# The later chunks' scores head by head, with the three products of the split parts stacked in one contraction of 120 rows

## The chip, the cores and the metric

The kernel runs on one core of a Trainium2 chip. The metric is the device time of one execution in microseconds (us). Before the change three timed executions gave 582.05 us as the median, from 581.89 to 585.11. A change of 1% (5.8 us) or more is called faster or slower here.

The engines are named as in the profile: PE is TensorE (PEld its weight loads), DVE is VectorE, ACT is ScalarE, POOL is GpSimd, and SP is SyncE, which here issues nearly all DMA transfers.

## The reference

The program is an mLSTM layer followed by a gated feed-forward layer (FFN). Batch is 4, heads 8, sequence 768, head width 40; the FFN goes from 320 to 1536 and back.

```python
for t in range(S):                        # per batch and head
    m_new  = maximum(f_gate[t] + m, i_gate[t])
    f_stab = exp(f_gate[t] + m - m_new);  i_stab = exp(i_gate[t] - m_new);  m = m_new
    C = f_stab * C + i_stab * outer(v[t], k[t])
    n = f_stab * n + i_stab * k[t]
    y[t] = sigmoid(o_gate[t]) * (C @ q[t]) / maximum(abs(n . q[t]), 1.0)
x   = y.transpose(0, 2, 1, 3).reshape(B * S, H * D)      # 3072 x 320
out = (sigmoid(x @ w_gate) * (x @ w_val)) @ w_out
```

The weights arrive as 64-bit floats, and the kernel decodes them on the chip.

## The kernel before, in words

The sequence is cut into 6 chunks of 128 steps. A chunk of one batch row is a unit, so there are 24 units, written (chunk, row). Within a unit the recurrence is a masked attention: the scores are k against q over the 40 columns of a head, multiplied by a matrix of decays `d` (128 x 8 heads x 128), and `av` is their product with v. Between chunks the state C goes on in `cst`; its share of a unit's output is `in`, its update `cs`. When the four units of a chunk are done, their rows `xh`/`xl` go through the FFN: `pg` (two products, up) and `po` (down), in 12 slices of 128 of the 1536. The FFN of a chunk runs while the units of the next chunk are worked on, so PE's queue is a mixture of both.

A unit has five stages. `st_a` transposes q and k on PE into PSUM (`pt`, three groups of 3, 3 and 2 heads, so 120, 120 and 80 partitions) and prepares the operands of the scores. `st_b` makes the scores `s` and multiplies them into `d`. `st_c` makes `in`, `av` and the normalisation, `st_d` transposes the result for the FFN (`xt`), and `st_e` updates the state. The next loads of q, k, v, o and d are issued in `prefetch`, after `st_c` and `st_e` of a unit.

Accuracy is got by splitting numbers: a float32 value is a high part in the format fp32r, which PE multiplies in one pass, and a low part, the rest. A product of two split numbers is high by high, low by high and high by low. Chunks 0 and 1 make their scores in plain float32 (line 405 of the profile). Chunks 2 to 5, 16 units, use the split: `kh` (ACT, L374) and `kl` (DVE, L375) hold both transposed operands. Since a group holds three heads on 120 partitions, the q side is spread into a block matrix with zeros by a mask, `bh` on DVE and `bl` on POOL (L382), 384 or 256 columns wide; three products per group, nine per unit, add up in PSUM (L413).

The order of the work is written out in numbers: `PARAM['pos']` gives each stage and each weight step a position in units of FFN slices, `PARAM['open']` does so for the opening (chunk 0, rows 0 and 1). Events are issued in the order of these positions, and stages a to d with a small priority over the FFN work around them. Each engine's queue is executed in its order; a wait at its head holds what stands behind.

Buffers that matter: `kh`, `kl`, `bh` and `bl` exist once each, q, k, v, o and `d` three times, the two PSUM banks `pa` serve all of a unit's products.

Of the kernel before, what the change touches and what calls it, by code (L numbers as in the profile page):

```python
# [9 lines left out]
F32 = mybir.dt.float32  # L10
F32R = mybir.dt.float32r
# [42 lines left out]
    'ce': -6.41,  # L54
    'open': {
# [9 lines left out]
        'xt0': 66.039, 'wve': 68.058, 'wrb': 58.626, 'nb1': 61.591, 'wrc': 61.877, 'xt1': 48.778, 'wrd': 70.574,  # L65
        'wre': 69.0, 'kw1': 69.362, 'e2': 87.005,
# [7 lines left out]
def mlstm_then_gated_ffn_kernel(  # L74
# [15 lines left out]
    P = 128  # L90
# [251 lines left out]
    def st_a(c, b):  # L342
# [21 lines left out]
        kh = two.tile([P, 3, 2, L], F32R, tag="kh", name=f"kh_{c}_{b}", bufs=1)  # L364
        kl = two.tile([P, 3, 2, L], F32R, tag="kl", name=f"kl_{c}_{b}", bufs=1)
        bh = two.tile([P, 3, 3, L], F32R, tag="bh", name=f"bh_{c}_{b}", bufs=1)
        bl = two.tile([P, 3, 3, L], F32R, tag="bl", name=f"bl_{c}_{b}", bufs=1)
        sop[u] = kh, kl, bh, bl
        for g, (h0, nh) in enumerate(GROUPS):
# [4 lines left out]
            nc.scalar.activation(kh[:r, g], pt[:r], AF.Copy)  # L374
            nc.vector.tensor_tensor(kl[:r, g], pt[:r], kh[:r, g].bitcast(F32), ALU.subtract)  # L375
            if c > 0:
                if PARAM["eng"].get(f"qk{g}") == "a":
                    nc.scalar.activation(qk[u][:r, g], pt[:r, 0], AF.Copy)
                else:
                    nc.vector.tensor_copy(qk[u][:r, g], pt[:r, 0])  # L380
            for eng, src, dst in ((E(f'bh{g}'), kh, bh), (E(f'bl{g}'), kl, bl)):
                eng.tensor_tensor(dst[:r, g, :nh, :],  # L382
                                        src[:r, g, 0, :].bitcast(F32).unsqueeze(1).broadcast_to([r, nh, L]),
                                        bmask[:r, :nh, :], ALU.mult)
# [514 lines left out]
```

## Time and profile before

| | value |
|---|---|
| timed executions, median (range) | 582.05 us (581.89 to 585.11) |
| the profiled execution's own time | 587.93 us |
| its span, first to last instruction | 586.2 us |
| granted PE clock, mean | 0.98 |
| instructions | 9768 |
| PE, PEld busy | 555.0 us, 506.0 us |
| DVE, ACT, POOL busy | 370.9, 234.3, 213.3 us |
| DMA moved | 43.91 MB, mean 75 GB/s |

The profile is one execution. A matmul's end is modelled, and matmuls are pipelined: one that lasts 0.34 us in a row may be followed 0.18 us later by the next. What one costs PE is therefore read from the start of one row to the start of the next. A row of the timeline gives start, duration, engine, line, operation, what it writes and reads, shapes, and a count where equal rows were merged. In rows of groups the two numbers after the bar are the busy time of the group in us and the mean of one in ns; then come idle time before them and what ended it. A float32 product shows as two instructions, an fp32r product as one.

### The profile page before, as it was taken

Reading aid. Unit: us, or ns where it says so; the run is one execution under the profiler, and the core shown is the slowest. Engines: PE = TensorE matmul, PEld = TensorE weight load, DVE = VectorE, ACT = ScalarE, POOL = GpSimd, SP = SyncE. Lnnn points to the kernel's source line nnn. Section 1 sums busy time; section 2 is a strip of 40 time slices with the busy share of each in tenths; the row PEclk is TensorE's granted clock in tenths of the full one; section 3 lists DMA queues with packets and bytes.
Section 4 is the critical chain, followed back from the end, with each engine's and each line's share of the span. In section 5 each row is a group of like instructions: output and inputs, shape, how many; then the busy total and the mean of one; then the engine's idle time right before and its main releaser. Section 6 shows DMA issues by size and latency. Waiting matters only on the chain.

```text
span 586.2 us, 9768 instructions
## 1 busy us (share of the span) xinstructions
PE 555.0 (95%) x3601; PEld 506.0 (86%) x3601; DVE 370.9 (63%) x780; ACT 234.3 (40%) x580; POOL 213.3 (36%) x279
## 2 busy tenths in 40 slices
PE   8639989899999999999999999999999999999997
PEld 7528878688999998999888988898888889999996
DVE  4697877966446786665767656676656767533322
ACT  5375757445335334343332342333342322223222
POOL 5566644654234543533445323445312321000000
PEclk9777999999999999999999999999999999999999
DMA  9875765322403405312030523030423000010000
GB/s 200 238 180 154 172 206 129 93 82 46 112 15 77 109 13 130 81 45 70 13 82 11 128 64 74 13 82 13 119 66 81 1 1 1 0 46 1 25 1 22
DMA packets 112847, 43.91 MB, mean 75 GB/s; under 512 B 101280, under 2 KB 104544, under 8 KB 112800
## 3 DMA queue, kind: packets, MB, share of 16 engines
q1 hardware_dynamic: 111712, 43.04, 30.0%
q8 instruction: 28, 0.46, 0.3%
q10 hardware_dynamic: 1088, 0.26, 0.2%
q14 instruction: 19, 0.16, 0.1%
HBM read 39.26 MB, written 4.03 MB: 74 GB/s over the span
## 4 chain that ended last, share of the span: by engine, by line
PE 80%; DVE 9%; DMA 3%; ACT 3%; POOL 2%; issue 2%; POOLq 0%; ACTq 0%; DVEq 0%
PE pg L509 31%; PE po L533 7%; PE po L532 7%; PE po L531 6%; PE av L429 5%; PE pg L511 5%; PE pg L514 5%; PE s L413 4%; DMA st_o<-in_moe_w_out_dram 2%; PE in L424 2%; PE pt L373 2%; PE cs L477 2%; DVE dc L266 2%; DVE dc L261 1%; PE xt L465 1%
## 5 line engine op out<-in xcount | busy, mean ns | idle before, releaser
L509 PE MATMUL pg<-xh,wh 128*128 128x256 f32 (+1 forms) x412 | 116.8, 350 | 3.8 <-ACT sg L516 2.2
L516 ACT ACTIVATE sg<-pg 128x256 f32<-128x256 f32 (+1 forms) x103 | 48.2, 468 | 169.9 <-PE pg L514 169.2
L517 DVE SCALAR_TENSOR_TENSOR sg<-sg,pg 128x256 f32<-128x256 f32 (+1 forms) x103 | 53.9, 523 | 97.6 <-ACT sg L516 93.1
L509 PE MATMUL pg<-xh,wl 128*128 128x256 f32 (+1 forms) x412 | 112.1, 342 | 0.0
L509 PE MATMUL pg<-xl,wh 128*128 128x256 f32 (+1 forms) x412 | 107.6, 334 | 0.0
L532 PE MATMUL po<-ol,gh 128*128 128x320 f32 x288 | 96.7, 336 | 0.0
L533 PE MATMUL po<-oh,gl 128*128 128x320 f32 x288 | 95.0, 330 | 0.0
L531 PE MATMUL po<-oh,gh 128*128 128x320 f32 x288 | 94.2, 327 | 0.4 <-ACT gh L520 0.4
L509 PEld LDWEIGHTS pg<-xh,wh 128*128 128x128 f32 x412 | 71.5, 192 | 11.0 <-ACT sg L516 3.8
L521 DVE TENSOR_TENSOR gl<-sg,gh 128x256 fp32r<-128x256 f32 (+1 forms) x103 | 62.5, 607 | 27.7 <-ACT gh L520 26.9
L509 PEld LDWEIGHTS pg<-xl,wh 128*128 128x128 f32 x412 | 70.9, 191 | 7.1
L509 PEld LDWEIGHTS pg<-xh,wl 128*128 128x128 f32 x412 | 70.8, 192 | 6.6
L520 ACT ACTIVATE gh<-sg 128x256 fp32r<-128x256 f32 (+1 forms) x103 | 51.7, 502 | 46.6 <-DVE sg L517 46.2
L382 POOL TENSOR_TENSOR bl<-kl,bmask 120x384 fp32r<-120x384 f32 (+1 forms) x48 | 50.3, 1056 | 54.7 <-DVE kl L375 54.7
L531 PEld LDWEIGHTS po<-oh,gh 128*128 128x128 f32 x288 | 54.7, 190 | 3.2 <-ACT gh L520 0.6
L532 PEld LDWEIGHTS po<-ol,gh 128*128 128x128 f32 x288 | 54.6, 190 | 0.9 <-issue 0.3
L533 PEld LDWEIGHTS po<-oh,gl 128*128 128x128 f32 x288 | 54.3, 189 | 0.5 <-DVE gl L521 0.2
L429 PEld LDWEIGHTS av<-v,d 128*128 128x128 f32 x352 | 52.7, 192 | 1.5 <-PE in L424 0.9
L511 PE MATMUL pg<-xh,w 128*128 128x256 f32 (+1 forms) x206 | 52.8, 332 | 0.0
L514 PE MATMUL pg<-xl,w 128*128 128x256 f32 (+1 forms) x206 | 52.3, 332 | 0.0
L429 PE MATMUL av<-v,d 128*128 128x41 f32 x352 | 50.7, 254 | 0.8 <-issue 0.8
L382 DVE TENSOR_TENSOR bh<-kh,bmask 120x384 fp32r<-120x384 f32 (+1 forms) x48 | 46.3, 965 | 0.0
(134 smaller groups left out, 914.2 us busy)
## 6 DMA issues: line engine op xcount, KB each, us to landing
d<-mscr SPq DMA_DIRECT2D x22, 512.0 KB, 3.8
k<-in_k_dram SPq DMA_DIRECT2D x24, 160.0 KB, 3.3
v<-in_v_dram SPq DMA_DIRECT2D x24, 160.0 KB, 3.6
o<-in_o_gate_dram SPq DMA_DIRECT2D x24, 160.0 KB, 3.7
st_o<-in_moe_w_out_dram SPq DMA_DIRECT2D x12, 320.0 KB, 3.2
out_dram<-ob SPq DMA_DIRECT2D x24, 160.0 KB, 1.8
q<-in_q_dram SPq DMA_DIRECT2D x23, 160.0 KB, 2.5
st<-in_moe_w_gate_dram SPq DMA_DIRECT2D x6, 512.0 KB, 4.5
```

The lines of the kernel that those rows point to most:

```text
L382: eng.tensor_tensor(dst[:r, g, :nh, :], src[:r, g, 0, :].bitcast(F32).unsqueeze(1).broadcast_to([r, nh, L]), bmask[:r, :nh, :], ALU.mult)
L429: nc.tensor.matmul(pv[:, h, :], dm[u][:, h, :], vt[u][:, h, :], start=True, stop=True)
L509: nc.tensor.matmul(pg[n], w[n][:, a, fs], x[c][:, a, n0:n1], start=(i + a == 0), stop=False)
L511: nc.tensor.matmul(pg[n], w2[n][:, fs], xh[c][:, 2, n0:n1], start=False, stop=False)
L514: nc.tensor.matmul(pg[n], w2[n][:, fs], xl[c][:, 2, n0:n1], start=False, stop=True)
L516: nc.scalar.activation(sg, pg[0], AF.Tanh, scale=0.5)
L517: nc.vector.scalar_tensor_tensor(sg, sg, 1.0, pg[1], ALU.add, ALU.mult)
L520: last = nc.scalar.activation(gh[u][:, :nt], sg, AF.Copy)
L521: E('gl0' if c == 0 else 'gl').tensor_tensor(gl[u][:, :nt], sg, gh[u][:, :nt].bitcast(F32), ALU.subtract)
L531: nc.tensor.matmul(po[t], g1[:, ts], oh[:, j, :], start=(j == 0), stop=False)
L532: nc.tensor.matmul(po[t], g1[:, ts], ol[:, j, :], start=False, stop=False)
L533: nc.tensor.matmul(po[t], g0[:, ts], oh[:, j, :], start=False, stop=(j == NF - 1))
```

## The change: what it does

For chunks 2 to 5 the block matrices are no longer made. `kh` and `kl` are laid out with the operand (q or k) ahead of the group. Two new tiles, `ks` and `qs`, are filled by DMA from SBUF to SBUF: for a head, 40 partitions of the high part of k, below them the same 40 again, below them 40 of the low part; for q the order is high, low, high. One product over 120 partitions then gives high by high plus high by low plus low by high. It is 128 columns wide, one per head, eight per unit. The transfers are 18 per unit (three parts, three places of a head in its group, two operands), 40 partitions by 1536 or 1024 bytes, all issued by SP.

```diff
 PARAM = {
     'pos': {
-        'e0': -11.132, 'a0': -4.375, 'b0': -13.304, 'a1': -17.116, 'e1': -7.942, 'c0': -10.313, 'd0': -8.526, 'b1':
+        'e0': -4.126, 'a0': -3.256, 'b0': -13.366, 'a1': -17.116, 'e1': -6.935, 'c0': -10.823, 'd0': -9.886, 'b1':
...
-    'ce': -6.41,
+    'ce': -3.09,
...
-        kh = two.tile([P, 3, 2, L], F32R, tag="kh", name=f"kh_{c}_{b}", bufs=1)
-        kl = two.tile([P, 3, 2, L], F32R, tag="kl", name=f"kl_{c}_{b}", bufs=1)
-        bh = two.tile([P, 3, 3, L], F32R, tag="bh", name=f"bh_{c}_{b}", bufs=1)
-        bl = two.tile([P, 3, 3, L], F32R, tag="bl", name=f"bl_{c}_{b}", bufs=1)
-        sop[u] = kh, kl, bh, bl
+        kh = two.tile([P, 2, 3, L], F32R, tag="kh", name=f"kh_{c}_{b}", bufs=1)
+        kl = two.tile([P, 2, 3, L], F32R, tag="kl", name=f"kl_{c}_{b}", bufs=1)
         for g, (h0, nh) in enumerate(GROUPS):
...
-            nc.scalar.activation(kh[:r, g], pt[:r], AF.Copy)
-            nc.vector.tensor_tensor(kl[:r, g], pt[:r], kh[:r, g].bitcast(F32), ALU.subtract)
...
-            for eng, src, dst in ((E(f'bh{g}'), kh, bh), (E(f'bl{g}'), kl, bl)):
-                eng.tensor_tensor(dst[:r, g, :nh, :],
-                                        src[:r, g, 0, :].bitcast(F32).unsqueeze(1).broadcast_to([r, nh, L]),
-                                        bmask[:r, :nh, :], ALU.mult)
+            nc.scalar.activation(kh[:r, :, g, :], pt[:r], AF.Copy)
+            nc.vector.tensor_tensor(kl[:r, :, g, :], pt[:r], kh[:r, :, g, :].bitcast(F32), ALU.subtract)
...
+        ks = two.tile([P, H, L], F32R, tag="bh", name=f"ks_{c}_{b}", bufs=1)
+        qs = two.tile([P, H, L], F32R, tag="bl", name=f"qs_{c}_{b}", bufs=1)
+        sop[u] = ks, qs
+        for x, dst, parts in ((1, ks, (kh, kh, kl)), (0, qs, (kh, kl, kh))):
+            for i, p in enumerate(parts):
+                for m in range(3):
+                    ng = len(range(m, H, 3))
+                    nc.sync.dma_start(dst[i * D : (i + 1) * D, 3 * m : 3 * m + ng, :].bitcast(F32),
+                                      p[m * D : (m + 1) * D, x, :ng, :].bitcast(F32))
...
-        kh, kl, bh, bl = sop.pop(u)
+        ks, qs = sop.pop(u)
         for g, (h0, nh) in enumerate(GROUPS):
-            r = nh * D
             ps = bank(c, b, [P, 3, L], f"s_{g}")
-            for i, (x, y) in enumerate(((kh, bh), (kl, bh), (kh, bl))):
-                nc.tensor.matmul(ps[:, :nh, :], x[:r, g, 1, :], y[:r, g, :nh, :], start=(i == 0), stop=(i == 2))
+            for m in range(nh):
+                nc.tensor.matmul(ps[:, m, :], ks[: 3 * D, 3 * m + g, :], qs[: 3 * D, 3 * m + g, :], start=True, stop=True)
```

Most numbers of `pos` and `open` are others too, so the order moves everywhere. In what follows a name's last number tells buffers apart, the numbers ahead of it are chunk and row (for `pg` chunk, slice and first row).

PE's queue before, at the scores of unit (4,3), amid the up products of slice 10:

```order
L509 MATMUL pg_3_10_0_4683<-xh_3361,wh_99 128x512
L477 MATMUL cs_2_4626<-v_2_3859,k_2_3858 120x123
L413 MATMUL s_4_3_4655<-bh_3_4535,kh_3_4533 128x384
L413 MATMUL s_4_3_4655<-bh_3_4535,kl_3_4534 128x384
L413 MATMUL s_4_3_4655<-bl_3_4536,kh_3_4533 128x384
L509 MATMUL pg_3_10_0_4683<-xh_3361,wh_99 128x512
```

The same place now:

```order
L510 MATMUL pg_3_10_0_4814<-xl_3652,wh_96 128x512
L414 MATMUL s_4_3_4788<-qs_3_4638,ks_3_4637 128x128
L414 MATMUL s_4_3_4793<-qs_3_4638,ks_3_4637 128x128
L414 MATMUL s_4_3_4788<-qs_3_4638,ks_3_4637 128x128
L414 MATMUL s_4_3_4793<-qs_3_4638,ks_3_4637 128x128
L510 MATMUL pg_3_10_0_4814<-xl_3652,wh_96 128x512
```

Three products of 384 columns made one group; now two groups are made in turn, head by head. Between the last `pt` of this unit and its first score stand 24 products `po`, 21 `pg` and the `in`, `av` and `cs` of unit (4,2).

DVE's queue before, in stage a of unit (4,0):

```order
L375 TENSOR_TENSOR kl_0_4008<-pt_4_0_4011,kh_0_4007 120x256
L380 COPY qk_0_4006<-pt_4_0_4011 120x128
L382 TENSOR_TENSOR bh_0_4009<-kh_0_4007,bmask 120x384
L521 TENSOR_TENSOR gl_1_0_4003<-sg_1_0_3999,gh_1_0_4002 128x512
L375 TENSOR_TENSOR kl_0_4008<-pt_4_0_4019,kh_0_4007 120x256
```

And now:

```order
L372 TENSOR_TENSOR kl_0_4047<-pt_4_0_4048,kh_0_4046 120x2x128
L538 TENSOR_SCALAR ob_0_4089<-po_2_3126 128x320
L376 COPY qk_0_4045<-pt_4_0_4048 120x128
L522 TENSOR_TENSOR gl_0_0_4039<-sg_0_0_4035,gh_0_0_4038 128x512
L372 TENSOR_TENSOR kl_0_4047<-pt_4_0_4054,kh_0_4046 120x2x128
```

The product with the mask is gone from the row of steps between one group and the next.

SP's queue before, where the output rows `ob` of chunk 2 leave:

```order
L133 DMA v_2_3859<-in_v_dram 128x8x40
L541 DMA out_dram<-ob_1_3966 128x320
L541 DMA out_dram<-ob_0_3960 128x320
L541 DMA out_dram<-ob_2_3972 128x320
L541 DMA out_dram<-ob_3_3978 128x320
L131 DMA q_3_4134<-in_q_dram 128x8x40
```

And now, with the transfers of unit (4,0):

```order
L133 DMA v_2_3947<-in_v_dram 128x8x40
L385 DMA ks_0_4066<-kh_0_4046 40x256 x2
L542 DMA out_dram<-ob_0_4089 128x320
L385 DMA qs_0_4067<-kh_0_4046 40x256
L542 DMA out_dram<-ob_1_4095 128x320
L385 DMA ks_0_4066<-kh_0_4046 40x384 x3
L542 DMA out_dram<-ob_2_4101 128x320
L385 DMA ks_0_4066<-kh_0_4046 40x384
L542 DMA out_dram<-ob_3_4107 128x320
L385 DMA ks_0_4066<-kl_0_4047 40x384 x2
L385 DMA ks_0_4066<-kl_0_4047 40x256
L385 DMA qs_0_4067<-kh_0_4046 40x384 x2
```

Six more transfers to `qs` follow behind the piece shown, and the load of q of unit (4,3) comes after them. In this unit the output's transfers stand among the new ones; in most others the 18 stand in a block.

More of the change, by code (lines that the diff above doesn't have):

```diff
@@ L53 @@
     'pin': 2.71,
-    'ce': -6.41,
+    'ce': -3.09,
     'open': {
[9 rows of a table removed]
-        'xt0': 66.039, 'wve': 68.058, 'wrb': 58.626, 'nb1': 61.591, 'wrc': 61.877, 'xt1': 48.778, 'wrd': 70.574,
-        'wre': 69.0, 'kw1': 69.362, 'e2': 87.005,
[9 rows of a table added]
+        72.38, 'xt0': 65.463, 'wve': 69.125, 'wrb': 54.301, 'nb1': 62.627, 'wrc': 63.052, 'xt1': 50.168, 'wrd':
+        71.641, 'wre': 79.377, 'kw1': 70.535, 'e2': 88.072,
     },
@@ L373, in st_a @@
                 nc.tensor.transpose(pt[:r, x, :], t[u][:, h0 : h0 + nh, :].rearrange("p h d -> p (h d)"), ident)
[L374 to L380, printed above, removed]
-            for eng, src, dst in ((E(f'bh{g}'), kh, bh), (E(f'bl{g}'), kl, bl)):
-                eng.tensor_tensor(dst[:r, g, :nh, :],
-                                        src[:r, g, 0, :].bitcast(F32).unsqueeze(1).broadcast_to([r, nh, L]),
-                                        bmask[:r, :nh, :], ALU.mult)
+            nc.scalar.activation(kh[:r, :, g, :], pt[:r], AF.Copy)
+            nc.vector.tensor_tensor(kl[:r, :, g, :], pt[:r], kh[:r, :, g, :].bitcast(F32), ALU.subtract)
+            if PARAM["eng"].get(f"qk{g}") == "a":
+                nc.scalar.activation(qk[u][:r, g], pt[:r, 0], AF.Copy)
+            else:
+                nc.vector.tensor_copy(qk[u][:r, g], pt[:r, 0])
+        ks = two.tile([P, H, L], F32R, tag="bh", name=f"ks_{c}_{b}", bufs=1)
[7 more added lines that the diff above has]
+                                      p[m * D : (m + 1) * D, x, :ng, :].bitcast(F32))
     dlast = {}
```

46 rows, old and new, of the table PARAM are left out of this document.

## The prediction

> **What bounds the kernel now.** I read the busy shares and the chain first. In the chain the columns are shares of the span.
>
> ```profile
> PE 555.0 (95%) x3601; PEld 506.0 (86%) x3601; DVE 370.9 (63%) x780; ACT 234.3 (40%) x580; POOL 213.3 (36%) x279
> PE 80%; DVE 9%; DMA 3%; ACT 3%; POOL 2%; issue 2%; POOLq 0%; ACTq 0%; DVEq 0%
> PE pg L509 31%; PE po L533 7%; PE po L532 7%; PE po L531 6%; PE av L429 5%; PE pg L511 5%; PE pg L514 5%; PE s L413 4%; DMA st_o<-in_moe_w_out_dram 2%; PE in L424 2%; PE pt L373 2%; PE cs L477 2%; DVE dc L266 2%; DVE dc L261 1%; PE xt L465 1%
> ```
>
> PE carries 80% of the path; the scores to be changed (L413) are 4% of it, 23.4 of 586.2 us, or 1.46 us for each of 16 units. DVE's 9% must lie somewhere, so the busy times by stretch come next; the columns are start and end, length, then busy time per engine, granted clock, DMA share and GB/s.
>
> ```profile
> 30.00:40.00 10.00, 2.92 (x20) 2.07 (x19) 9.62 (x22) 7.73 (x28) 4.36 (x8) 0.84 0.92 210
> 50.00:100.00 50.00, 47.00 (x304) 40.72 (x304) 40.12 (x93) 33.06 (x91) 24.86 (x32) 1.00 0.65 170
> 100.00:150.00 50.00, 47.38 (x275) 40.93 (x274) 33.90 (x65) 25.50 (x61) 27.15 (x29) 1.00 0.32 83
> 190.00:250.00 60.00, 56.34 (x426) 54.55 (x425) 44.35 (x106) 21.67 (x61) 29.59 (x39) 0.97 0.36 83
> 250.00:300.00 50.00, 50.00 (x334) 46.10 (x334) 32.07 (x72) 18.20 (x42) 19.29 (x24) 1.00 0.18 41
> 300.00:400.00 100.00, 99.85 (x585) 88.41 (x584) 64.79 (x127) 36.13 (x81) 39.11 (x49) 1.00 0.27 65
> 400.00:500.00 100.00, 100.00 (x589) 88.96 (x589) 69.19 (x132) 31.73 (x66) 28.90 (x34) 1.00 0.18 41
> ```
>
> From 250 to 500 us PE is busy 249.85 of 250 us: there only less work on PE shortens anything. From 190 to 250 it stands idle 3.66 us at a clock of 0.97. In the opening DVE is full (9.62 of 10) and PE mostly waits. The waits of PE in 200 to 250, and the opening's largest, are (us in total, times, longest):
>
> ```profile
> PE s L413 <- DVE xl L468: 1.3, 1, 1.3
> PE s L413 <- DVE qk L380: 0.9, 1, 0.9
> PE xt L465 <- DVE qk L380: 0.7, 1, 0.7
> PE pt L354 <- ACT cst L489: 4.8, 2, 3.7
> ```
>
> **The scores on PE.** What a product costs PE is the step from its start to the next start. This stretch at 442 us has no gaps (start, duration):
>
> ```profile
> 439.73 0.62 PE L509 MATMUL pg<-xh,wh 128*128 128x512 f32 x2
> 440.19 0.63 PE L509 MATMUL pg<-xh,wl 128*128 128x512 f32 x2
> ...
> 442.06 0.34 PE L413 MATMUL s<-bh,kh 120*128 120x384 f32 x1
> 442.24 0.31 PE L531 MATMUL po<-oh,gh 128*128 128x320 f32 x1
> 442.39 0.34 PE L413 MATMUL s<-bh,kl 120*128 120x384 f32 x1
> 442.57 0.31 PE L532 MATMUL po<-ol,gh 128*128 128x320 f32 x1
> ...
> 444.18 0.29 PE L413 MATMUL s<-bh,kh 80*128 80x256 f32 x1
> 444.31 0.31 PE L532 MATMUL po<-ol,gh 128*128 128x320 f32 x1
> ...
> 445.40 0.90 PE L424 MATMUL in<-cst,qk 120*128 120x123 f32 x6
> 446.14 1.92 PE L429 MATMUL av<-v,d 128*128 128x41 f32 x16
> 447.88 0.71 PE L509 MATMUL pg<-xh,wh 128*128 128x512 f32 x2
> ```
>
> A score product of 384 columns costs 0.18 us (442.06 to 442.24), one of 256 some 0.125, `po` 0.15, `pg` of 512 columns 0.23. A unit's nine are 6 x 0.18 + 3 x 0.125 = 1.455 us, which agrees with the chain's 1.46. The new product, 128 columns with a weight load of its own each time, does not occur in fp32r. Two bounds: by columns alone, the step from 384 to 256 saves 0.055, so 128 would cost 0.07; among small products, sixteen of 41 columns take 1.74 us, 0.109 each, and six of `in` (123 and 82 columns) 0.74 us, 0.123 each. Three times fewer columns cost the same there, so columns do not set it; each brings new weights. I take 0.11, from the nearest in kind: 8 x 0.11 = 0.88 us. Saved: 0.575 us per unit, times 16, **-9.2 us**, all on the path. At 0.07 it is -14.3. [...]
>
> **DVE and POOL.** Gone with the masks, per unit (mean ns before the last bar):
>
> ```profile
> L382 POOL TENSOR_TENSOR bl<-kl,bmask 120x384 fp32r<-120x384 f32 x32 | 37.8, 1184 | 49.8 <-DVE kl L375 49.8
> L382 DVE TENSOR_TENSOR bh<-kh,bmask 120x384 fp32r<-120x384 f32 x32 | 33.8, 1057 | 0.0
> L382 DVE TENSOR_TENSOR bh<-kh,bmask 80x256 fp32r<-80x256 f32 x16 | 12.5, 783 | 0.0
> ```
>
> DVE loses 2 x 1.06 + 0.78 = 2.9 us and POOL about 3.2 us per unit. After 250 us that buys nothing, since PE does not wait. Before it, the three waits above (2.9 us) end on DVE steps that stand behind `bh`, and the lower clock costs 0.03 x 60 = 1.8 us. At most 4.7 us come back; at least nothing, if the waits pass to ACT. I take **-2.5**. `kh`, `kl` and `qk` stay, at the same sizes.
>
> **The transfers.** A unit's path from `pt` to the scores now runs through 18 issues of SP. Nearest rows, for a transpose, `kh`, an ACT step that can stand ahead of it, SP's spacing and the landing (KB over all issues, then us):
>
> ```profile
> L373 PE MATMUL pt<-ident,k 128*80 128x128 f32 x16 | 4.3, 271 | 0.0
> L374 ACT ACTIVATE kh<-pt 80x256 fp32r<-80x256 f32 x16 | 6.0, 375 | 8.6 <-PE pt L373 8.6
> L227 ACT ACTIVATE d<-d 128x1024 f32<-128x1024 f32 x16 | 16.7, 1047 | 1.3 <-POOL d L226 1.3
> 302.13 0.37 SPq L132 DMA_DIRECT2D k<-in_k_dram  x1
> 302.55 0.69 SPq L133 DMA_DIRECT2D v<-in_v_dram  x1
> 38.38 2.24 SPq L169 DMA_DIRECT2D mscr<-mg  x4
> d<-mscr SPq DMA_DIRECT2D x22, 512.0 KB, 3.8
> out_dram<-ob SPq DMA_DIRECT2D x24, 160.0 KB, 1.8
> ```
>
> The first issue comes 0.65 us after the start of the last transpose (0.27 + 0.375), 1.7 us with the ACT step ahead. `kl` follows on DVE while the first six, from `kh`, are issued. Seventeen steps of 0.42 us (302.13 to 302.55) are 7.1. Landing is between 1.8 (160 KB) and 3.8 us (512 KB); these carry 61 KB or 41 KB. The whole is 9.6 to 12.6 us. Cover: for unit (4,3), 24 `po`, 21 `pg` of 512 columns and unit (4,2)'s `in`, `av` and `cs` (28 instructions at about 0.11) stand between, 24 x 0.15 + 21 x 0.23 + 28 x 0.115 = 11.6 us. Counted so, all 16 gaps are 11.3 to 15.5 us, ten of them at 12.2 or less. A chain of 9.6 is hidden; one of 12.6 leaves about 8 us of waits in all. I take **+2**, mostly for rows 0 of chunks 3 to 5, whose transfers share SP with the outputs. Queued behind SP's waits are loads for later units, which are not needed before the next units begin, and the outputs; an output that leaves late holds one of two buffers that `ob` shares with `t1`, and so DVE and ACT, which is why these rows 0 are where I put the waits.
>
> [...]
>
> **The order.** Stages a of chunk 2 start about three slices earlier within chunk 1, which is needed for the longer path. In the opening the transposes of unit (0,2), which wait 4.8 us above for a PSUM bank, now stand behind the gates' transposes; DVE stays full, so I take **-1**, between -4.8 and +4.
>
> **Sum.** -9.2 - 2.5 + 2 - 1 = -10.7 us. The profiled execution took 587.93 us (span 586.2) and would take 577.2. The median of the timed ones is 582.05, 5.9 us below it; the difference is carried over: **571.4 us**.
>
> **The rivals.**
>
> *Cheaper products.* At 0.07 the scores give -14.3: 566.3 us. For it: weight loads overlap with a long `pg` ahead. Against: the 0.109 of `av`. [...] Chance 0.15.
>
> *Late transfers (slower).* If SP spaces its issues as in the opening's row of four (2.24 us, 0.56 each, at a DMA share of 0.92), and ACT delays the first and landing takes 3.8, the path is 1.7 + 17 x 0.56 + 3.8 = 15.0 us, and the 16 gaps leave about 40 us of waits; with a landing of 1.8, a path of 13.0 us, about 13 us. It decides from 12.7 us of waits on (all gains but the transfers' own term), 0.8 per unit, a path of about 13 us. For it: nothing is spare in the ten short gaps. Against: a DMA share of 0.18 to 0.36 there. The time is 582.05 - 12.7 + 13 = 582 to 609; I take the middle of the lower half, 592. Chance 0.12.
>
> *Dear products.* If PE takes fp32r of 128 columns as it takes float32, two steps of 0.123 (`in`), a unit costs 8 x 0.246 = 1.97, +8.2 us instead of -9.2: 588.8. For it: nothing of this width in one pass is in the trace. Against: 384 to 256 columns scale as expected. Chance 0.10.
>
> *Gain given back early.* Chunk 2's units now fall into the stretch 50 to 150 us as well, where PE already idles 5.6 us; if that doubles, 577. Chance 0.15.
>
> That the change doesn't do what it says is excluded: the queue shows 128 products of 128 columns and no mask step.
>
> **How the numbers follow.** The forecast has 0.48 (566 to 577). Faster by over 1% means below 576.2: nearly all of the forecast, the cheap products, a quarter of the last rival, 0.64. Slower means above 587.9: most of the late transfers, half of the dear products, 0.13. Within 1%: 0.23. The range goes from 562 (cheap products, all 4.7 us of DVE's waits, no wait for transfers: 566.3 - 2.2 - 2) to 587, leaving out about 0.05 below and 0.14 above.
>
> **What would show it.** Right: `s` (L414) steps of 0.11 us, 14 us of the chain; no masks; PE busy in nearly all of 250 to 500 us; no wait of `s` on a DMA above 1 us; last `qs` landing within 11 us of the last `pt`. Wrong: `s` waiting on `qs` or `ks` in many units, SP spacing above 0.5 us, or steps of 0.07 or 0.2 us.

## The result, and the profile after

| | before | after |
|---|---|---|
| median of 4 runs, us | 582.99 (581.89 to 585.11) | 650.33 (644.31 to 653.5) |
| ratio, with 95% interval | | 1.114 (1.104 to 1.123) |
| profiled execution, us (span) | 587.93 (586.2) | 652.26 (650.5) |
| PE busy, us | 555.0 | 585.4 |
| PE idle in the span, us | 31.2 | 65.1 |
| mean granted clock | 0.980 | 0.924 |

The forecast was 571.4 us, and the kernel became 67 us slower. The profile splits the 64.3 us between the spans into two nearly equal halves: PE stands idle 33.9 us longer, and it is busy 30.4 us longer, although it has less to compute. Some executions of a kernel take over 1.5% more than its fastest; the ratios in this document leave these out, the medians do not.

The page of the changed kernel, busy time, clock by slice and the chain's shares by engine and by line:

```profile
PE 585.4 (90%) x3585; PEld 528.3 (81%) x3585; DVE 324.5 (50%) x732; ACT 232.6 (36%) x580; POOL 158.0 (24%) x231
PEclk9669999999979988778898996989898989899999
PE 50%; SPq 17%; DVE 11%; DMA 9%; ACT 5%; issue 4%; POOL 4%; ACTq 0%; POOLq 0%; DVEq 0%
PE pg L510 18%; SPq L385 17%; PE av L430 4%; DMA qs<-kh 4%; PE po L534 4%; PE po L532 3%; PE po L533 3%; PE pg L512 3%; PE s L414 3%; PE pg L515 3%; PE in L425 2%; PE pt L370 2%; DMA st_o<-in_moe_w_out_dram 2%; DVE dc L266 1%; DMA o<-in_o_gate_dram 1%
```

PE's share of the chain fell from 80% to 50%; SP's issuing of the new transfers (L385) took 17%, and their landing (`qs<-kh`) 4%. Relief came where it was forecast and buys nothing: DVE is busy 324.5 us instead of 370.9, POOL 158.0 instead of 213.3.

The stretches, with the columns as before (start and end, length, busy time of PE, PEld, DVE, ACT and POOL, granted clock, DMA share, GB/s):

```profile
190.00:250.00 60.00, 55.52 (x410) 53.06 (x410) 30.89 (x81) 20.93 (x58) 14.81 (x22) 0.94 0.42 106
250.00:300.00 50.00, 44.86 (x261) 43.93 (x260) 18.36 (x51) 12.97 (x36) 7.27 (x12) 0.73 0.30 81
300.00:400.00 100.00, 91.81 (x495) 79.18 (x493) 42.60 (x92) 29.02 (x63) 18.88 (x30) 0.94 0.31 84
400.00:500.00 100.00, 92.52 (x499) 79.86 (x498) 44.83 (x98) 31.19 (x70) 18.96 (x28) 0.92 0.34 92
```

From 250 to 500 us PE was busy 249.85 us at full clock before; now it is busy 229.19 us, at a clock between 0.73 and 0.94. The waits of PE from 165 us on (us in total, times, longest):

```profile
PE s L414 <- DMA qs<-kh: 24.1, 15, 3.7
PE s L414 <- issue: 7.0, 5, 2.4
```

Thirteen of the sixteen later units wait at their first score product, for 1.4 to 3.7 us. What they wait for is SP. Its issues of the end of unit (4,0) (start, duration):

```profile
385.36 2.25 SPq L385 DMA_DIRECT2D ks<-kl  x3
387.65 1.46 SPq L385 DMA_DIRECT2D qs<-kh  x2
389.15 2.21 SPq L385 DMA_DIRECT2D qs<-kl  x3
391.41 2.21 SPq L385 DMA_DIRECT2D qs<-kh  x3
393.72 0.42 SPq L131 DMA_DIRECT2D q<-in_q_dram  x1
```

Three new transfers take 2.25 us (389.15 to 391.41 for three), 0.75 us each, while the load of q behind them takes 0.42. The 18 of a unit take 13.5 us. In all sixteen units the first score product stands 13.0 to 16.3 us behind the last transpose.

And what the clock does after such a wait; the stretch around unit (3,0)'s scores, in windows of 3 us:

```profile
281.00:284.00 3.00, 2.52 (x20) 2.31 (x18) 0.85 (x2) 0.80 (x2) 0.00 (x0) 1.00 0.21 75
284.00:287.00 3.00, 0.46 (x3) 0.49 (x3) 0.00 (x0) 0.00 (x0) 0.00 (x0) 0.77 0.22 77
287.00:290.00 3.00, 3.00 (x15) 3.00 (x16) 1.07 (x3) 0.39 (x1) 0.00 (x0) 0.50 0.35 67
...
296.00:299.00 3.00, 3.00 (x12) 2.66 (x12) 2.12 (x8) 1.51 (x6) 0.51 (x3) 0.50 0.90 254
299.00:302.00 3.00, 3.00 (x16) 2.39 (x15) 1.24 (x4) 0.76 (x2) 1.74 (x1) 0.96 0.52 85
```

PE waits 3.0 us and then works at a clock of 0.50 until 299 us, which costs another 6.4 us (half of the 12.7 us from 286.5 on). From 150 us on there are 14 idle stretches of 1.4 to 3.7 us, and 12 of them are followed by such a stretch, from 3.4 to 14 us long; together these cost some 36 us. Before, there was one stretch at half clock after 150 us, of 3.4 us.

### The profile page after: what moved, and what is told of

Same layout as the page of the kernel before. It is cut to its first block, busy times and chain, and to the rows that moved or that the text cites. A ratio compares the mean times of both kernels' runs of the same rounds, so it can differ in the third digit from the quotient of the medians.

```text
span 650.5 us, 10100 instructions
## 1 busy us (share of the span) xinstructions
PE 585.4 (90%) x3585; PEld 528.3 (81%) x3585; DVE 324.5 (50%) x732; ACT 232.6 (36%) x580; POOL 158.0 (24%) x231
## 4 chain that ended last, share of the span: by engine, by line
PE 50%; SPq 17%; DVE 11%; DMA 9%; ACT 5%; issue 4%; POOL 4%; ACTq 0%; POOLq 0%; DVEq 0%
PE pg L510 18%; SPq L385 17%; PE av L430 4%; DMA qs<-kh 4%; PE po L534 4%; PE po L532 3%; PE po L533 3%; PE pg L512 3%; PE s L414 3%; PE pg L515 3%; PE in L425 2%; PE pt L370 2%; DMA st_o<-in_moe_w_out_dram 2%; DVE dc L266 1%; DMA o<-in_o_gate_dram 1%
## 5 line engine op out<-in xcount | busy, mean ns | idle before, releaser
L510 PE MATMUL pg<-xh,wl 128*128 128x256 f32 (+1 forms) x412 | 119.2, 358 | 0.0
L510 PE MATMUL pg<-xl,wh 128*128 128x256 f32 (+1 forms) x412 | 115.5, 350 | 0.0
L522 DVE TENSOR_TENSOR gl<-sg,gh 128x256 fp32r<-128x256 f32 (+1 forms) x103 | 65.8, 639 | 35.3 <-ACT gh L521 34.9
L510 PEld LDWEIGHTS pg<-xh,wl 128*128 128x128 f32 x412 | 73.7, 199 | 6.0
L510 PEld LDWEIGHTS pg<-xl,wh 128*128 128x128 f32 x412 | 73.0, 198 | 5.7
L430 PEld LDWEIGHTS av<-v,d 128*128 128x128 f32 x352 | 59.6, 211 | 4.5 <-DVE t L427 0.9
L414 PEld LDWEIGHTS s<-qs,ks 120*128 120x128 f32 x128 | 25.2, 235 | 41.3 <-issue 37.8
L414 PE MATMUL s<-qs,ks 120*128 120x128 f32 x128 | 29.5, 322 | 31.7 <-DMA qs<-kh 24.1
L534 PEld LDWEIGHTS po<-oh,gl 128*128 128x128 f32 x288 | 56.1, 195 | 0.6 <-DVE gl L522 0.3
L430 PE MATMUL av<-v,d 128*128 128x41 f32 x352 | 54.1, 272 | 0.7 <-DVE t L427 0.7
```

Source lines behind the costliest of these rows:

```text
L414: nc.tensor.matmul(ps[:, m, :], ks[: 3 * D, 3 * m + g, :], qs[: 3 * D, 3 * m + g, :], start=True, stop=True)
L430: nc.tensor.matmul(pv[:, h, :], dm[u][:, h, :], vt[u][:, h, :], start=True, stop=True)
L510: nc.tensor.matmul(pg[n], w[n][:, a, fs], x[c][:, a, n0:n1], start=(i + a == 0), stop=False)
L522: E('gl0' if c == 0 else 'gl').tensor_tensor(gl[u][:, :nt], sg, gh[u][:, :nt].bitcast(F32), ALU.subtract)
L534: nc.tensor.matmul(po[t], g0[:, ts], oh[:, j, :], start=False, stop=(j == NF - 1))
```

## The experiments

Theory 1, formed from these lines: SP needs 0.75 us for each transfer where I took 0.42, so that the path is longer than the gap that the order leaves, PE waits, and each wait brings half clock. The rivals: the products of 128 columns or the new order are dear in themselves; or the transfers cost by what they hold up, and not by PE's wait for the last one. Ratios below are against the kernel before, run beside each variant. The order that a table of positions gives also depends on the instructions in it: less PE's waits, the scores of the changed kernel stand 11.2 to 15.2 us behind the last transpose, those of the products alone, with the same table, 0.4 to 18.4 us.

### The products alone

```diff
-        ks = two.tile(...);  qs = two.tile(...);  18 x nc.sync.dma_start(...)
+        sop[u] = kh
...
-                nc.tensor.matmul(ps[:, m, :], ks[: 3 * D, 3 * m + g, :], qs[: 3 * D, 3 * m + g, :], start=True, stop=True)
+                nc.tensor.matmul(ps[:, m, :], kh[: nh * D, 1, g, :], kh[: nh * D, 0, g, :], start=True, stop=True)
```

> The changed kernel without the eighteen transfers: the eight products of 128 columns read the transposed high parts where they lie (contraction over the 120, 120 and 80 rows of a group), so the low parts and the separation by head are left out of the scores. Theory 1 (the transfers arrive too late, because SP needs 0.707 us to issue one where I took 0.42 for the spacing, and PE stands waiting): without them the rest of my sum holds, 582 less 9.2 (products), 2.5 (masks) and 1 (order), that is 569 us, 563 to 577, and PE's busy time from 250 to 500 us is back at 249 of 250 us. Rival, dear products or a dear new order: the time stays above 590 us, since neither is touched. By the step between products this run also settles their price: 0.11 us each by my sum, 0.07 or 0.246 at its ends.

Measured: ratio 1.002 (0.996 to 1.008); median 590.8 us against 586.1, with ten executions from 581 to 595 us. Without the transfers nearly the whole loss is gone, so they carry some 11%. But my sum without them, 569, is missed as well: theory 1 is right on the transfers, and something else takes back what the products save. The next two runs separate that.

### The order alone, and the products in the old order

The first is the kernel before with the changed kernel's table of positions, the second the products alone with the table of the kernel before. Neither changes any other line.

> The kernel before with the changed kernel's table of positions: nine products, masks, no transfers, only the new order. The products alone took some 590 us (most of its runs), not my 569, and what it lost it lost before 200 us: PE was busy 125.2 of the first 150 us against 127.4 before, at a clock of 0.80, 0.97 and 0.93 against 0.80, 1.00 and 1.00. Theory A (the new order costs some 10 us by itself, in the opening): 588 to 597 us, with the same rows up to 150 us. Theory B (the order is neutral and the eight products are no cheaper than the nine): 580 to 587 us.

> The products alone (eight products from the transposed high parts, no transfers; low parts and separation by head left out), in the order of the kernel before. Five products in a row took 0.74 us there, 0.148 each, others 0.125, so that a unit costs 1.0 to 1.2 us instead of 1.455. Theory A (the order costs, the products gain 4 to 7 us and the masks 2): 572 to 580 us. Theory B (the products gain nothing): 581 to 588 us.

Measured: the order alone 1.021 (1.017 to 1.025), 597.25 us against 584.62; the products in the old order 0.991 (0.988 to 0.994), 580.2 us. Theory A holds in both. The order, which I had put at -1 us, costs 12.6 us. Where is only half answered: from 250 to 560 us PE now waits 5.0 us in all, against 0.15 before, and the first 150 us ran at 0.78, 0.98 and 0.97 of the clock instead of 0.80, 1.00 and 1.00.

```profile
PE pg L509 <- DVE sg L517: 4.0, 5, 1.6
```

The products' price can be read in the second run, at full clock and without a gap (start, duration):

```profile
474.46 0.23 PE L406 MATMUL s<-kh 120*128 120x128 f32 x1
474.52 0.36 PE L526 MATMUL po<-oh,gl 128*128 128x320 f32 x1
474.72 0.23 PE L406 MATMUL s<-kh 120*128 120x128 f32 x1
474.78 0.45 PE L502 MATMUL pg<-xh,wh 128*128 128x512 f32 x1
475.06 0.22 PE L406 MATMUL s<-kh 120*128 120x128 f32 x1
```

A score product and a `pg` take 0.34 us (474.72 to 475.06), a score product and a `po` 0.26; less 0.23 and 0.15, that leaves 0.11 us, the value taken. In the changed kernel most of them stand in pairs, where the step from one to the next is 0.13 us (median of 42 at full clock). In the second run PE's busy time fell by 9.1 us, from 555.0 to 545.9, as the term of -9.2 has it. Of these only 4.4 us arrive in the time. The rest shows: between 250 and 500 us PE stands idle 4.6 us, where it was 0.15 before, and most of that it waits for DVE to empty a bank of PSUM.

```profile
PE pt L370 <- DVE d L407: 2.0, 3, 0.7
PE in L417 <- DVE d L407: 1.2, 2, 0.7
```

### The transfers, read by nobody

```diff
-        sop[u] = ks, qs
+        sop[u] = kh
```

with the score products of the products alone.

> As the products alone, but with the eighteen transfers of each later unit issued where the changed kernel issues them; nothing reads what they bring, so that the scores again leave out the low parts and the separation by head. Theory 1 (only PE's wait for the last transfer costs): within 1.5% of the products alone, about 569 to 578 us, although SP is occupied as long as in the changed kernel, 16 times 13.5 us. Rival (the transfers cost by what they hold up: loads and stores queued behind them on SP, DMA engines, access to SBUF): at least half of the 67 us is still there, 615 to 650 us.

Measured: 1.038 (1.030 to 1.045), 612.8 us: neither within 1.5% of the products alone nor half of the loss. Of the 11% that the transfers cost, 3.6% remain when nobody waits for what they bring. They read `kh` and `kl`, of which there is one buffer each, so the next unit's copies on ACT wait for them; PE's transposes then wait 9.8 us in all for a bank that DVE empties behind these copies. What ACT's copies into `kh` (L371) waited for:

```profile
  DMA qs<-kh: 25.9, 5
```

I had left this wait out: in the changed kernel the scores' own wait comes first and hides it. The loads behind the transfers on SP come late as well, as the rival had it: ACT waits 22.6 us for `o` (5.2 in the products alone), POOL 31.9 us for `d` (20.3).

### Thirty-two rows

```diff
-                    nc.sync.dma_start(dst[i * D : (i + 1) * D, ...], p[m * D : (m + 1) * D, ...])
+                    nc.sync.dma_start(dst[i * 32 : (i + 1) * 32, ...], p[m * D : m * D + 32, ...])
```

> The changed kernel with 32 of the 40 rows of each part carried, put at rows 0, 32 and 64, and products over 96 rows: 8 of the 40 columns of each head are left out of the scores. As many transfers, four fifths of their bytes, the same waits. Theory 1 with the row count as the reason for SP's price (a count that 16 divides is issued in 0.35 us, as the 128-row loads are): spacing about 0.42 us, path 18 x 0.42 + 2 = 9.6 us, below the 11 to 15 us between a unit's transposes and its scores, PE's waits for the transfers mostly gone, 570 to 590 us. Rivals (the price belongs to any transfer within SBUF, to the number of pieces, or the lateness is in the landing): issue stays at 0.7 us, 635 to 655 us.

Measured: 1.033 (1.028 to 1.038), 607.1 us, and neither expectation: the issue fell, but to 0.59 us, not to 0.35. SP's issues in this kernel (ns, least, median and most):

```profile
L385 SPq DMA_DIRECT2D ks<-kh x96: 507/582/1462, 172.9 to 506.5; - x96
```

At 0.63 us from issue to issue the path is 18 x 0.63 + 2 = 13.3 us, 2.2 us shorter, and the kernel is 43 us faster: 2.7 us for each of 16 units. PE still waits for the transfers, but 10.5 us in all instead of 31.1, and half clock costs some 9 us instead of 36. So the path's length is what counts, and a little of it decides much.

### What an issue costs

To the products alone, six transfers were added in each later unit, a different form in each.

> The products alone, with six transfers from a constant in SBUF added to SP's queue in each of the sixteen later units, one form per unit: 40, 32, 48, 64, 80, 96, 120, 128, 16, 20, 8 rows of 384 numbers, 40 and 128 rows of 128, 24 rows and 41 rows of 384, and 40 rows of 40 from device memory; nothing reads them, and the scores leave out the low parts and the separation by head. If the row count sets the price: 0.33 to 0.42 us for 16, 32, 48, 64, 80, 96 and 128 rows, some 0.7 us for 40, 20, 8, 24, 120 and 41, whatever the length of a row or the memory. If the size does: the price rises with the bytes from 40 x 128 to 128 x 384. If any transfer within SBUF is dear: 0.7 us for all but the one from device memory. Time: within 2% of the products alone.

Measured: 590.7 us, and these prices (ns), for 16, 128, 8, 40, 120 and 41 rows of 384 numbers from SBUF, 40 rows of 128 from SBUF, and 40 rows of 40 from device memory:

```profile
L352 SPq DMA_DIRECT2D zi<-bmask x6: 536/584/588, 215.5 to 219.9; - x6
L352 SPq DMA_DIRECT2D zh<-bmask x6: 471/600/2757, 203.4 to 215.0; - x6
L352 SPq DMA_DIRECT2D zk<-bmask x6: 624/624/649, 229.1 to 232.6; - x6
L352 SPq DMA_DIRECT2D za<-bmask x6: 718/756/897, 147.0 to 160.5; - x6
L352 SPq DMA_DIRECT2D zg<-bmask x6: 792/816/858, 190.2 to 199.3; - x6
L352 SPq DMA_DIRECT2D zp<-bmask x6: 565/996/2679, 250.1 to 256.2; - x6
L352 SPq DMA_DIRECT2D zl<-bmask x6: 717/723/756, 233.4 to 237.3; - x6
L352 SPq DMA_DIRECT2D zo<-in_k_dram x6: 282/332/440, 247.5 to 249.5; - x6
```

For comparison, the output rows in the kernel before, which go from SBUF to device memory, 128 at a time:

```profile
L541 SPq DMA_DIRECT2D out_dram<-ob x24: 332/356/1198, 146.0 to 583.1; - x24
```

Two things add up. A transfer from SBUF to SBUF is issued in 0.58 to 0.60 us (medians) for 16, 32 and 128 rows, against 0.33 for one from device memory even with 40 rows and 0.36 for one to device memory. So a source in SBUF alone is not dear; both ends lie there in the dear ones. Other row counts took more: 0.62 us with 8 rows, 0.76 with 40, 0.82 with 120 and 1.0 with 41; in the kernels themselves 40 rows take 0.12 us more than 32 (0.707 against 0.587). The length of the rows hardly counts (0.723 for 128 numbers, 0.756 for 384). Why a transfer with both ends in SBUF is dearer, and why the row count has a price, these runs do not show.

### A wider gap, and a second queue

Three runs leave the computation whole and attack the lateness: positions that put the scores about 20 us behind the transposes in the plan; nine transfers on ACT's queue; nine on POOL's queue.

```diff
-        'as0': 0.239, 'bs0': 8.575, 'as1': 2.501, 'bs1': 5.915, ...                                            # wide gap
+        'as0': 0.25, 'bs0': 3.0, 'as1': 3.05, 'bs1': 5.8, ...
...
-                    nc.sync.dma_start(dst[...], p[...])
+                    (nc.scalar if p is kh and x == 0 or i == 0 else nc.sync).dma_start(dst[...], p[...])   # ACT
+                    (nc.gpsimd if x == 0 else nc.sync).dma_start(dst[...], p[...])                         # POOL
```

> The changed kernel, complete, with other positions for the four steps of the units of chunk 2 on: a unit's scores stand some 2.5 FFN steps, 20 us, behind its transposes, where they stood 11 to 16. The transfers keep their price: 18 issues at 0.75 us and 2.1 us for the last to land make 15.6 us. Theory 1 (PE waits because that path is longer than the gap, and each wait of 2 us or more is followed by a stretch at half the clock): the waits for transfers and the half-clock stretches go, 578 to 595 us. Rival (the transfers cost by contention or by what they hold up in SP's queue): 610 us or more, with waits in other places.

> The changed kernel, complete, with nine of the eighteen transfers of a unit (those of the high parts that come first) issued by ACT and nine by SP. Theory 1: two queues halve the path to 9 x 0.75 + 2 = 8.8 us, below every gap; the waits for transfers go, and with them the half-clock stretches, 580 to 597 us. Rival (the issues hold up ACT's own work, 9 x 0.7 = 6.3 us for each unit on an engine at 36%, or the transfers' landing is the limit): 605 us or more, with PE waiting for ACT or still for the transfers.

> The changed kernel, complete, with the nine transfers of q issued by POOL and the nine of k by SP. With ACT as the second queue PE waited for ACT's own work (pg for sg: 24.8 us); POOL is busy 24% and PE rarely waits for it. Theory 1 (a queue of its own that delays nobody): path 9 x 0.75 + 2 = 8.8 us, 585 to 602 us. Rival (POOL's issue is dearer, or the decay matrices and norms that POOL makes come late behind it): 615 us or more.

Measured: wide gap 1.078 (1.071 to 1.084), ACT 1.085 (1.080 to 1.089), POOL 1.028 (1.018 to 1.038; 602.5 us). Only POOL comes close to what was expected of all three.

The plan's 20 us did not arrive whole: less the waits, the scores stand 11.7 to 20.6 us behind the transposes, thirteen of sixteen at 13.5 or more. PE waits less for transfers (9.5 us instead of 31.1), but the wait has moved. The chain of one such move, on POOL, ACT and PE:

```profile
329.93 1.90 POOL L395 TENSOR_TENSOR d<-at,d 128x1024 f32<-128x1024 f32 x1 [6.87 <-DMA d<-mscr]
331.86 1.06 ACT L396 ACTIVATE d<-d 128x1024 f32<-128x1024 f32 x1 [3.46 <-POOL d L395]
332.82 0.37 ACT L540 ACTIVATE kh<-pt 120x256 fp32r<-120x256 f32 x1
333.99 0.44 PE L539 MATMUL pt<-ident,q 128*120 128x128 f32 x1 [3.57 <-DVE qk L545]
```

The load of the decay matrix `d` was issued at 324.96, behind a unit's 18 transfers on SP; POOL and ACT were late with it, the copies of the next unit stood behind ACT's exponential, and PE waited 3.6 us for a bank. With ACT as the second queue PE waits for ACT's own work, 24.8 us in 13 waits (in an execution of 643 us, where the other three took 633 to 637), since the issues stand in ACT's program ahead of `sg`:

```profile
PE pg L510 <- ACT sg L517: 24.8, 13, 3.6
```

POOL issues in 0.51 us, and nothing urgent stands behind it; PE's waits for transfers fall from 31.1 to 7.3 us, although less the waits the scores now stand only 5.7 to 9.9 us behind the transposes in thirteen of sixteen units:

```profile
L385 POOL DMA_DIRECT2D qs<-kh x96: 512/512/708, 171.8 to 502.8; - x96
```

So, as far as these runs show, the length of SP's queue is the cause, by the last transfer in the changed order and by what stands behind the transfers in the others.

### Fewer transfers, and the change in the old order

```diff
-            for i, p in enumerate(parts):
+            for i, p in enumerate(parts[:1]):      # six transfers;  parts[:2]: twelve
```

> The changed kernel with six of a unit's eighteen transfers, those of the first part (high times high): products over 40 rows, so the two products with a low part are left out. Path 6 x 0.75 + 2.1 = 6.6 us. Theory 1 (PE waits only where the path is longer than the gap, and a wait of some 2 us brings half clock): no wait of 1.5 us for transfers, no half clock, and the time is that of the products alone in this order, 585 to 597 us. Rival (each transfer costs, by the hold-up in SP's queue and in SBUF: 60 us for 18, so 3.3 us for each of a unit): about 610 us.

> As before with twelve transfers, those of the first two parts, and products over 80 rows (the product of the low part of k is left out). Path 12 x 0.75 + 2.1 = 11.1 us. Theory 1: still below or at the gaps of 11 to 15 us that the changed kernel's order leaves, few waits, 588 to 605 us. Rival, so much for each transfer: about 630 us.

> The change in the order of the kernel before. There the transposes stood 2.6 to 14.5 us ahead of the scores, 8.5 on the mean of sixteen. Theory 1 (path 15.6 us): 16 x 7 = 113 us of waits for transfers and 5 us at half clock behind each, 730 to 790 us. Rival (the program's order is made with the transfers in view, and the table only shifts it a little): 640 to 670 us, as with the new order.

Measured: six 633.3 us (1.081, 1.071 to 1.091), twelve 608.7 and 619.1 us in two executions, the old order 677.6 us in one execution. Six being dearer than twelve fits no theory, and the waits don't explain it: PE waits for transfers 1.8 us in all. The products over 40 rows are dear themselves, here at full clock (start, duration):

```profile
473.05 0.32 PE L414 MATMUL s<-qs,ks 40*128 40x128 f32 x1
473.30 0.41 PE L532 MATMUL po<-oh,gh 128*128 128x320 f32 x1
473.64 0.32 PE L414 MATMUL s<-qs,ks 40*128 40x128 f32 x1
```

A product of 40 rows and a `po` take 0.59 us where one of 120 rows and a `po` took 0.26: 0.33 us more. That holds for the 76 of 128 that stand alone between products over 128 rows; from one 40-row product to the next the step is 0.14 us. So it explains some 25 us of the 42 us to the products alone. Half clock costs some 22 us more, with 49 us of it from 150 us on, against 5 in the products alone (which lose some 6 us more by idle time and in the opening). Yet PE hardly waits in this kernel (busy times, clock and DMA as above):

```profile
400.00:500.00 100.00, 99.17 (x508) 82.17 (x507) 45.56 (x100) 30.17 (x65) 18.14 (x29) 0.93 0.26 66
```

Four of its six stretches at half clock from 150 to 600 us begin with no idle time of PE shown in the 3 us ahead of them, so what theory 1 says of waits is not all that brings half clock. This run says nothing on the number of transfers.

With twelve (80 rows; in the products in the old order a score product of 80 rows and a `pg` took 0.34 us, as with 120 rows) there are waits of up to 1.8 us, 12.2 in all, and the time lies above the expected 588 to 605. The gaps had moved: less the waits, they are 8.0 to 9.8 us in thirteen units, shorter than the path of 11.1, and not the 11 to 15 that I took over.

In the old order the waits are 40 us and half clock costs 53 us: the rival was nearer, for there too the program moves the scores away from the transposes, to 10.6 us or more (less the waits) in fifteen of sixteen units, where twelve of sixteen stand under 10 us in the kernel before. The new order is better for the transfers, and dearer without them.

### Does a wait alone bring half clock?

In the kernel before, with no transfers and no new product, PE is held up at eight places by a chain of copies on ACT:

```diff
+        nc.tensor.transpose(d1[:, 0, :], ident, ident)
+        nc.scalar.activation(scr, d1[:, 0, :], AF.Copy)
+        for _ in range(n - 1):
+            nc.scalar.activation(scr, scr, AF.Copy)
+        held = nc.tensor.transpose(d1[:, 1, :], scr, ident)     # the FFN's next products are put behind it
```

> The kernel before, with PE held up at eight places of chunks 3 to 5: a small product there waits for a chain of 1, 10, 4, 14, 6, 12, 3 and 8 copies on ACT, some 0.25 us each, and the FFN's next products stand behind it. Theory (a wait of PE of about 2 us or more is itself followed by 4 to 15 us at half clock): each such hold shows a granted clock of 0.50 behind it, the shorter ones none, with no transfers in the kernel. Rival (the half clock in the changed kernel comes of something else: its thin products or its transfers): the clock stays at 1.00 behind every hold, and the time is 585 plus the holds alone.

> The same eight places with chains of 12, 3, 8, 2, 10, 5, 14 and 6 copies, so that long and short holds change places. Theory: the half clock goes with the length of the hold and not with the place. Rival: it stays at the places where it was, or is nowhere.

Measured: 623.9 and 617.5 us, in one execution each; a copy took some 0.29 us (2.34 us for ACT's eight instructions in 538 to 541 us of the first kernel). One hold of 4.0 us in the first kernel and one of 2.1 us in the second, each followed by the windows around it:

```profile
542.93 0.47 PE L512 MATMUL inj<-ident,scr 128*128 128x128 f32 x1 [4.01 <-ACT scr L511]
```

```profile
538.00:541.00 3.00, 0.92 (x7) 0.67 (x5) 1.03 (x2) 2.34 (x8) 0.00 (x0) 1.00 0.01 3
541.00:544.00 3.00, 1.07 (x5) 1.08 (x6) 0.00 (x0) 1.71 (x6) 0.00 (x0) 0.52 0.00 0
544.00:547.00 3.00, 3.00 (x16) 3.00 (x15) 0.00 (x0) 0.36 (x1) 0.00 (x0) 0.50 0.03 5
```

```profile
585.25 0.33 PE L512 MATMUL inj<-ident,scr 128*128 128x128 f32 x1 [2.13 <-ACT scr L511]
```

```profile
586.00:589.00 3.00, 3.00 (x16) 3.00 (x15) 0.14 (x1) 0.39 (x1) 0.00 (x0) 0.50 0.00 0
```

Half clock follows in a kernel that has none of the change, at places where the kernel before had full clock throughout: a wait alone is enough, and the rival falls. Counted over both kernels (idle time around a hold, which may lie in several pieces): behind the four holds with over 3 us there is half clock each time; behind those from 1.6 to 2.9 us four times of nine; behind the one of 1.1 us none. So longer waits bring it, but no sharp length decides: between 1.6 and 3 us it is a matter of when the wait falls. In all these traces the clock changes only at points that lie a multiple of 3.41 us apart, and a stretch at half clock costs 1.7 us or a multiple of it (3.4, 5.1, 6.8). The longest wait without half clock, 2.8 us in the first kernel, falls across such a point:

```profile
588.93:592.34 3.41, 2.43 (x20) 2.15 (x18) 1.15 (x3) 1.50 (x5) 0.00 (x0) 1.00 0.00 0
592.34:595.75 3.41, 1.57 (x13) 1.57 (x14) 0.00 (x0) 1.62 (x6) 0.00 (x0) 1.00 0.00 0
```

The 2.1 us in the second kernel lie whole between two points:

```profile
582.52:585.93 3.41, 1.27 (x11) 1.00 (x10) 0.78 (x2) 2.12 (x7) 0.00 (x0) 1.00 0.00 0
```

Counted over all eighteen traces, from 150 us on to 40 us before the end, among the intervals of 3.41 us at full clock: with 1.9 us of PE idle time or more inside, half clock followed in 39 of 39; with 1.0 to 1.9 us in 18 of 57; with less in 17 of 1613, of which 6 in the kernel with 40-row products.

### POOL's queue with the old order, and with a mixed one

Twelve transfers on POOL, six on SP; the first with the table of the kernel before, the second with its opening and its first half alone.

> The changed kernel, complete, in the order of the kernel before, with twelve of a unit's transfers (all of q, the first part of k) issued by POOL at 0.512 us and six by SP at 0.75. Path 12 x 0.512 + 2.6 = 8.7 us and 6 x 0.75 + 2.1 = 6.6 us. Theory (the changed kernel loses by SP's path, by what that path brings in half clock, and 12 us by its order; POOL's queue and the old order take all three away): no wait of 1.5 us for transfers, no half clock, 580 to 588 us, as the products alone in that order (580) and a little for POOL. Rival (in the old order the scores follow the transposes too closely, 8.5 us on the mean, so that some units wait still): 590 to 605 us.

> The same queues with a table of both: the opening and the positions up to the first unit of chunk 2 from the kernel before, those of the later units from the changed kernel. With nine transfers on POOL and the new table the kernel took 602 us; the new order by itself cost 12 us, which the products alone lost in the opening. Theory (the cost of the new order lies in its opening): 583 to 592 us. Rival (it lies in the later units): 595 to 603 us.

Measured: the old order 1.015 (1.009 to 1.022), 593.9 us; the mixed one 1.058 (1.053 to 1.063). Both expectations for the mixed order are missed: where the two tables meet, a unit waits 5.1 us for its transfers, and 38 us at half clock follow, in which PE is never full:

```profile
200.00:210.00 10.00, 7.04 (x32) 6.88 (x33) 2.06 (x5) 0.00 (x0) 1.65 (x4) 0.58 0.13 30
...
220.00:230.00 10.00, 7.23 (x32) 6.54 (x31) 5.65 (x11) 2.18 (x6) 7.46 (x11) 0.50 0.63 133
```

So it doesn't tell where the new order loses its 12 us. The other run is the best whole form of the change: with queue, order and most half clock taken out, 1.5% is left of 11.4%. Its time lies in the rival's range (590 to 605 us), and above the kernel before. But PE waits only 2.9 us for the transfers; the 14 us above the products alone in that order (580.2) are only in part explained, by some 4 us more of idle time from 150 us on and some 4 us of half clock. Since the products alone, without any transfer, reach 0.991, no way of carrying these operands can be expected to gain more than about 1% with that table.

## Why the prediction was wrong

The step that failed is the sizing of the transfers, "Seventeen steps of 0.42 us": the spacing was read from two loads from device memory. Measured: 0.75 us, so 13.5 us for the queue and 15.6 for the path where I had 9.6 to 12.6. The term, +2 us with a bound of +8, is in truth some 65 us (1.114 against 1.002 for the products alone).

Point by point:

- **What bounds the kernel.** Right as a reading of before: in 250 to 500 us only PE counts. It also means that PE had no slack to absorb any wait, which I did not turn round.
- **The scores on PE, -9.2 us.** Right in size: 0.11 us a product, PE busy 9.1 us less. But 4.4 us arrive, since a PE that is faster by this much waits for DVE (4.3 us between 250 and 500 us). The 0.07 us of the cheaper products is not borne out by these rows, nor are the 0.246 us of the dear ones.
- **DVE and POOL, -2.5 us.** The relief came (46 and 55 us of busy time); in the old order nothing of it can be told from the products' 4.4 us.
- **The gaps, 11.3 to 15.5 us.** Right. Less the waits, the scores begin 11.2 to 15.2 us behind the transposes.
- **The transfers.** Besides the spacing, the sum lacked a whole term: the clock. I let a wait cost its own length; in this kernel it costs about twice that, 31 us of waits and some 36 us of half clock. That the loads queued behind the transfers are not needed early did not hold either: ACT waits 28.7 us for `o` in the changed kernel (5.0 before). The sum had no price for 40 rows either: against 32 rows SP takes 0.12 us more an issue (0.707 against 0.587), 2.2 us a unit, and with what follows the kernel 43 us more (650.3 against 607.1).
- **The order, -1 us.** Wrong: +12.6 us by itself. I read the opening's transposes, and missed waits in the later part.
- **The rival of late transfers**, at 0.12, was the right mechanism, in the right place: its path of 15.0 us was measured as 15.6, its 40 us of waits as 31. It gave 592, or 609 at most, since it too had no price for the clock, and since it kept the other gains. Its evidence against, a low DMA share, was beside the point: in the changed kernel SP took 0.75 us a transfer at a share of 0.30 to 0.34 (250 to 500 us).

Of the three signs of an error named ahead, two came: scores that wait for `qs` in 13 of 16 units, and a spacing above 0.5 us. The third, another price of the products, did not.

## What to carry to other kernels

Price a queue by a row of the same form (both ends, row count), and where there is none, put the neighbours' difference into the range: here a transfer within SBUF cost 0.75 us where a load cost 0.42. Where PE is full, ask of every new wait not only how long it is but whether it reaches some 2 us, and then add the 1.7 us or more of half clock that it brings; in the changed kernel that doubled the waits. For a second queue ask what stands behind the transfers in its engine's program: with POOL, where it was nothing urgent, the kernel became 48 us faster, with ACT, where PE waited 24.8 us for `sg`, 15.

## What the runs showed of the hardware

- **Half clock after short waits.** In the changed kernel all seven idle stretches of 1.6 to 2.2 us were followed by clock 0.50 for 3.4 us or a multiple, and 12 of 14 between 1.4 and 3.7 us. What told best, over all the traces, was the idle time within one of the intervals of 3.41 us at whose ends the clock changes: with 1.9 us or more half clock followed in 39 of 39. And in the kernel with 40-row products it came four times behind intervals in which the profile shows PE without idle time.
- **An issue has a price by its two ends and its row count**: 0.33 us from device memory, 0.36 to it, 0.58 to 0.60 from SBUF to SBUF with 16, 32 or 128 rows, and there 0.62 with 8, 0.71 to 0.76 with 40, 0.82 with 120 and 1.0 with 41 rows, all on SP; 0.51 on POOL with 40. In the changed kernel the issues were 13.5 us of a unit's path of 15.6 us.
- **Products over 40 rows between products over 128** cost 0.33 us each beyond the 0.11 of 120 rows; from one 40-row product to the next the step was 0.14 us. No row shows why.
